# Fewer first-pass chunks for the first two token blocks, later key copies for a new batch, and 1 + exp(-|h|) on ScalarE

## The chip, the cores and the metric

The kernel runs on one core of one Trainium2 chip. A core has TensorE (PE in the profile, its weight loads PEld), VectorE (DVE), ScalarE (ACT), GpSimd (POOL) and SyncE (SP), and 16 DMA engines. Each engine takes its instructions from a queue of its own, in order, and waits on semaphores for what other engines and transfers make. The metric is the device time of one execution in microseconds (us), the median over the runs of a kernel.

## The reference, cut to what matters

Block-sparse attention (4 batches, 8 heads, 768 tokens of 64 elements) feeds a layer with a softplus. A block has 32 rows. A block of queries sees its neighbours, the first and the last block of keys, and three sampled ones; the first and the last block of queries see all keys.

```python
mask = np.abs(blk_i - blk_j) <= 1
mask |= (blk_i == 0) | (blk_j == 0) | (blk_i == n_blocks - 1) | (blk_j == n_blocks - 1)
# and mask[qb, kb] for the three sampled kb of each qb
attn = softmax(where(mask, q @ k.T / 8, -1e9))
x = (attn @ v)                       # 3072 tokens x 512
h = x @ w_in                         # 512 -> 2048
g = maximum(h, 0) + log1p(exp(-abs(h)))
out = g @ w_out                      # 2048 -> 512
```

All of it is in float32. The two weight matrices come as 8-byte numbers, which the kernel turns into float32 itself.

## The kernel before, in words

**Attention.** The tokens of a batch are six groups of 128 queries (three groups make a token block of 384, `GROUPS`, eight token blocks in all, `NTB`). Each group is a set; the queries that see all keys make one more set per batch, ahead of the batch's last group. A set has two units, so there are 28 sets and 56 units, 14 units a batch. A unit goes through scores (PE line 597, or 621 where all keys are seen), a masked minimum on VectorE (603 or 628), the exponents on ScalarE (653), transposes (666), copies of these out of PSUM (671 on VectorE, 673 on ScalarE), and values (696 or 710). In program order this is cut into three pieces a unit (`pieces`): score piece, value piece, transpose piece. `attend()` issues one piece and then calls `gather()` and `convert()`.

**Keys of a group.** The keys of a batch lie in `kT`, one buffer, so a batch's keys can be loaded only after the last scores of the batch before that read them. The score piece of the last all-keys unit issues the four loads of the next batch's keys (`load_kT`, line 427) and then `load_keys()`, which puts four entries (`of_block`) into `key_work`; each later `gather()` takes one of them. `of_block(0)` holds VectorE's copy of the neighbouring keys into the group's own buffer `kg` (line 493) and, for the first two groups of a batch, ScalarE's two copies of the first and the last key block (`end_keys`, line 476); each `of_block` also holds GpSimd's copies of the sampled blocks (507).

**The layer.** It runs in chunks: a chunk is one token block of 384 and one slice `f` of 128 of the 2048 hidden elements (`NF` is 16). Chunk n has 12 matmuls for h (lines 237 to 239), then |h| and exp(-|h|) on ScalarE (241, 242), `rounding` on VectorE (248: u = e + 1; 250 and 251 make max(h, 0) less what the sum lost), the logarithm on ScalarE (256), VectorE's sum (261), ScalarE's high part (265), VectorE's low part (271), and nine matmuls of `project` (293 to 295), `LEAD` = 3 chunks after h. There are 128 chunks in two passes. In the first pass (`phase` 0) every token block takes slices 0 to 5 (`EARLY`), among the pieces of the attention; the second pass takes all the other slices after it. `due` paces the pieces against the chunks: block t's chunks may begin when the attention of its three groups is issued, so the number of chunks of block 0 sets how many chunks stand between the attention of block 0 and that of block 1.

**Weights.** Each of the 32 halves (a slice of `w_in` or of `w_out`) is converted in steps spread over ticks, four ticks a half: ScalarE lines 155 and 159, VectorE 165, 172 and 178, GpSimd 182; the halves of slices 0 to 5 are also split into a high part (ScalarE 189) and a low part (VectorE 196) and stay in SBUF, the others are parked in memory. `convert()` adds to `owed` and does a tick whenever it reaches 1: one tick a call until the twelve early halves are through, half a tick a call from then on.

**What sets the order.** SyncE's queue follows the program text. For the other engines a scheduler orders the instructions by priority and by its own estimate of when each can start, except where `keep_in_program_order` pins one; so a change in the program text moves instructions on all of them.

## Time and profile before

| what | value |
|---|---|
| device time, median of 3 runs | 806.91 us (806.14 to 807.39) |
| device time of the profiled execution | 808.32 us |
| its span, first to last instruction | 806.6 us |
| TensorE busy | 777.5 us, 96% of the span |
| VectorE busy | 579.5 us, 72% |
| ScalarE busy | 490.0 us, 61% |
| GpSimd busy | 223.6 us, 28% |
| mean granted TensorE clock | 0.994 |

The profiled execution took 1.7 us more than its span and 1.4 us more than the median of the runs. A row of the view of groups gives an engine, a line of the kernel, the operation, out<-in by tile names, the count, then busy time and the mean of one in ns, and behind the bar the engine's idle time before these instructions and what ended it. A row of the view of windows gives a stretch from:to in us after the first instruction, its length, busy time and instructions (x) of PE, PEld, DVE, ACT and POOL, the granted clock, the DMA engines' busy share and GB/s. A row of the timeline gives start, length, engine, line, operation, and in brackets the idle time before it and what released it. The busy time of TensorE is modelled at its ends: a matmul that waits inside a run of others is counted as busy.

### The profile page before, as it was taken

What the parts mean: (1) busy time and instruction counts of PE and PEld (TensorE: products, weight loads), DVE (VectorE), ACT (ScalarE), POOL (GpSimd) and SP (SyncE); (2) the same over time, 40 slices, a digit from 0 to 9 for tenths busy, and PEclk for the clock granted to TensorE, in tenths of its full rate; (3) what the DMA queues carried; (4) which work ended last, traced back from release to release, by engine and by line L of the source; (5) the groups of instructions that cost most, each with busy time, mean ns of one, the idle gap of its engine ahead of it and who ended that gap; (6) DMA issues with size and microseconds to landing.
All of it is one profiled execution on the core that took longest, in us unless ns stands there. A gap on an engine that the chain in (4) does not pass through costs nothing.

```text
span 806.6 us, 21414 instructions
## 1 busy us (share of the span) xinstructions
PE 777.5 (96%) x8108; PEld 645.0 (80%) x8108; DVE 579.5 (72%) x1474; ACT 490.0 (61%) x1182; POOL 223.6 (28%) x389
## 2 busy tenths in 40 slices
PE   8788898998999999999999999999999999999997
PEld 7555666776777867778778999989999899988996
DVE  5689899887887888886756975656565656566564
ACT  4887886766877767767565764444444444444442
POOL 6874886625464436663000000000000000000000
PEclk9999999999999999999999999999999999999999
DMA  8999887886697786956415831203040313121021
GB/s 247 265 251 311 217 218 241 246 293 209 190 307 212 257 277 165 283 157 203 154 46 183 298 133 62 96 25 133 1 157 1 119 39 119 39 96 62 0 79 40
DMA packets 48407, 129.65 MB, mean 161 GB/s; under 512 B 5488, under 2 KB 5616, under 8 KB 46256
## 3 DMA queue, kind: packets, MB, share of 16 engines
q1 hardware_dynamic: 42304, 109.79, 42.7%
q0 software_dynamic: 5712, 17.57, 7.7%
q8 instruction: 64, 1.05, 0.5%
q10 hardware_dynamic: 288, 0.93, 0.3%
q14 instruction: 39, 0.32, 0.1%
HBM read 97.85 MB, written 30.41 MB: 159 GB/s over the span
## 4 chain that ended last, share of the span: by engine, by line
PE 72%; DVE 12%; ACT 9%; DMA 3%; issue 2%; SPq 1%; ACTq 0%; DVEq 0%
PE o L293 10%; PE h L237 10%; PE h L238 10%; PE o L294 10%; PE o L295 10%; PE h L239 10%; ACT pr L653 4%; PE t L666 4%; PE s L597 3%; PE x L696 3%; DMA kT<-in_k_dram 2%; DMA vg<-in_v_dram 2%; DVE e L250 2%; DVE pr L603 2%; DVE wt L178 1%
## 5 line engine op out<-in xcount | busy, mean ns | idle before, releaser
L237 PE MATMUL h<-x,w 128*128 128x384 f32 x512 | 176.5, 345 | 1.4 <-ACT pt L673 0.3
L238 PE MATMUL h<-x,w 128*128 128x384 f32 x512 | 172.5, 337 | 0.0
L239 PE MATMUL h<-x,w 128*128 128x384 f32 x512 | 172.4, 337 | 0.0
L293 PE MATMUL o<-w,gh 128*128 128x512 f32 x384 | 155.7, 405 | 0.0
L248 DVE TENSOR_SCALAR u<-e 128x384 f32<-128x384 f32 x128 | 49.6, 387 | 143.7 <-ACT e L242 143.4
L295 PE MATMUL o<-w,gl 128*128 128x512 f32 x384 | 152.4, 397 | 0.0
L294 PE MATMUL o<-w,gh 128*128 128x512 f32 x384 | 152.0, 396 | 0.0
L241 ACT ACTIVATE e<-h 128x384 f32<-128x384 f32 x128 | 62.5, 489 | 128.2 <-PE h L239 127.9
L653 ACT ACTIVATE pr<-pr,nmax 128x256 f32<-128x256 f32 (+2 forms) x208 | 110.3, 532 | 37.5 <-DVE nmax L603 24.3
L563 POOL DMA_INDIRECT vg<-in_v_dram,ix x88 | 90.1, 1023 | 69.2 <-PE x L696 38.0
L265 ACT CAST gh<-u 128x384 fp32r<-128x384 f32 x128 | 65.4, 511 | 69.9 <-PE o L294 69.2
L237 PEld LDWEIGHTS h<-x,w 128*128 128x128 f32 x512 | 96.1, 188 | 11.2 <-DVE nmax L628 2.2
L507 POOL COPY kg<-kT 128x128 f32 x252 | 88.4, 397 | 41.1 <-PE s L597 36.1
L238 PEld LDWEIGHTS h<-x,w 128*128 128x128 f32 x512 | 96.3, 188 | 3.7
L239 PEld LDWEIGHTS h<-x,w 128*128 128x128 f32 x512 | 96.1, 188 | 0.0
L256 ACT ACTIVATE u<-u 128x384 f32<-128x384 f32 x128 | 66.9, 523 | 42.8 <-DVE e L250 42.7
L293 PEld LDWEIGHTS o<-w,gh 128*128 128x128 f32 x384 | 72.1, 188 | 20.7 <-issue 8.6
L295 PEld LDWEIGHTS o<-w,gl 128*128 128x128 f32 x384 | 72.3, 188 | 17.3
L294 PEld LDWEIGHTS o<-w,gh 128*128 128x128 f32 x384 | 72.3, 188 | 13.5 <-issue 1.2
L250 DVE SCALAR_TENSOR_TENSOR e<-u,e 128x384 f32<-128x384 f32 x128 | 77.0, 602 | 3.6
L271 DVE TENSOR_TENSOR gl<-u,gh 128x384 fp32r<-128x384 f32 x128 | 73.2, 572 | 4.5 <-ACT gh L265 4.5
L261 DVE TENSOR_TENSOR u<-u,e 128x384 f32<-128x384 f32 x128 | 72.8, 569 | 3.4 <-ACT u L256 1.7
(81 smaller groups left out, 1082.4 us busy)
## 6 DMA issues: line engine op xcount, KB each, us to landing
vg<-in_v_dram SPq DMA_DIRECT2D x19, 768.0 KB, 6.4
xD<-x SPq DMA_DIRECT2D x8, 1536.0 KB, 7.1
x<-xD SPq DMA_DIRECT2D x8, 1536.0 KB, 6.3
raw<-in_w_in_dram SPq DMA_DIRECT2D x16, 512.0 KB, 9.9
raw<-in_w_out_dram SPq DMA_DIRECT2D x16, 512.0 KB, 8.5
qc<-in_q_dram SPq DMA_DIRECT2D x24, 256.0 KB, 7.1
vg<-in_v_dram SPq DMA_DIRECT2D x12, 512.0 KB, 5.9
yD<-os SPq DMA_DIRECT2D x24, 256.0 KB, 3.5
```

Source lines behind the costliest of these rows:

```text
L237: nc.tensor.matmul(ph, wh[:, cols], hi[:, c], start=(c == 0), stop=False)
L238: nc.tensor.matmul(ph, wh[:, cols], lo[:, c], start=False, stop=False)
L239: nc.tensor.matmul(ph, wl[:, cols], hi[:, c], start=False, stop=(c == NC - 1))
L250: nc.vector.scalar_tensor_tensor(out=e, in0=u, scalar=-1.0, in1=e, op0=ALU.add, op1=ALU.subtract)
L261: nc.vector.tensor_tensor(out=l, in0=l, in1=e, op=ALU.add)
L271: nc.vector.tensor_tensor(out=gl, in0=l, in1=G[n].bitcast(F32), op=ALU.subtract)
L293: nc.tensor.matmul(po[m], gh[:, cols], wh, start=first, stop=False)
L294: nc.tensor.matmul(po[m], gh[:, cols], wl, start=False, stop=False)
L295: nc.tensor.matmul(po[m], gl[:, cols], wh, start=False, stop=last)
L507: copy(out=kd[:, i, 1 + NR + s, :], in_=kT[b][:, bass.ds(x, 1), :].rearrange("p n f -> p (n f)"))
L563: nc.gpsimd.indirect_dma_start(out=vd[0 : 3 * BLOCK, 1, i, :], out_offset=None, in_=v, in_offset=bass.IndirectOffsetOnAxis(ap=ix[:, b, 4 * ...
L653: nc.scalar.activation(x, x, AF.Exp, bias=nmax[rows, r, j : j + 1], scale=-1.0, accum_out=rs[rows, h : h + 1])
```

## The change

Three edits and what they pull along. The first pass gives token block 0 four chunks (`EARLIEST`), block 1 five, and the other six blocks six each, 45 chunks in all where 48 stood; the second pass takes what is left, 83 chunks where 80 stood. The early weight halves are sorted by when this order wants them, and the early rate of conversion is 0.8 ticks a call, until 8 halves are through where 12 were. At a new batch three empty entries stand in `key_work` ahead of the first group's four, and the copies of the first and last key block go with the second entry instead of the first, pinned in program order. In `rounding`, u = 1 + e is made by an activation on ScalarE instead of VectorE's `tensor_scalar_add`.

```diff
+EARLIEST = 4
+ARRIVAL = 3
-EARLY_TICKS = 1.0
+EARLY_TICKS = 0.8
...
-    seq = [(0, t, f) for t in range(NTB) for f in range(EARLY)]
-    seq += [(1, t, f) for t in range(NTB) for f in range(EARLY, NF)]
+    early_of = [min(EARLY, EARLIEST + t) for t in range(NTB)]
+    steps = [sum(early_of[:t]) for t in range(NTB + 1)]
+    seq = [(0, t, f) for t in range(NTB) for f in range(early_of[t])]
+    seq += [(1, t, f) for t in range(NTB) for f in range(early_of[t], NF)]
...
-        nc.vector.tensor_scalar_add(out=u, in0=e, scalar1=1.0)
+        nc.scalar.activation(u, e, AF.Copy, bias=1.0)
...
-        first, last = (f == (0, EARLY)[phase]), (f == (EARLY, NF)[phase] - 1)
+        first, last = (f == (0, early_of[t])[phase]), (f == (early_of[t], NF)[phase] - 1)
...
-            copy(
+            ins = copy(
...
+            if m >= NG:
+                tc.keep_in_program_order(ins)
...
-                if m % NG < 2:
-                    first = nc.vector.tensor_copy if m == 0 else nc.scalar.copy
-                    end_keys(m, (first, nc.scalar.copy))
+            if m % NG < 2 and i == (m >= NG):
+                first = nc.vector.tensor_copy if m == 0 else nc.scalar.copy
+                end_keys(m, (first, nc.scalar.copy))
...
+        if g == 0 and b > 0:
+            key_work.extend((m, lambda: None) for _ in range(ARRIVAL))
...
-    early = sorted(((f, which) for f in range(EARLY) for which in range(2)), key=lambda x: (x[0] + LEAD * x[1], x[1]))
+    def wanted_at(f):
+        t = max(0, f + 1 - EARLIEST)
+        return steps[t] + f
+
+    early = sorted(
+        ((f, which) for f in range(EARLY) for which in range(2)), key=lambda x: (wanted_at(x[0]) + LEAD * x[1], x[1])
+    )
...
-    SECOND = NTB * EARLY
+    SECOND = steps[NTB]
...
-        owed += EARLY_TICKS if weights.at < 4 * len(early) + 9 else LATE_TICKS
+        owed += EARLY_TICKS if weights.at < 8 * EARLIEST + 9 else LATE_TICKS
...
-            end = t * EARLY - AHEAD
+            end = steps[t] - AHEAD
```

The change shifts the line numbers: lines 241, 242, 248, 250, 251, 256 of before are 248, 249, 255, 257, 258, 263 of after; 476 is 483, 493 is 502, 603 is 614, 653 is 664, 673 is 684; the weights' 155, 159, 165, 172, 178, 189, 196 are 159, 163, 169, 176, 182, 193, 200.

Three places show what the scheduler makes of it. First VectorE between the minimum of unit 14 (`nmax14`) and that of unit 15, in batch 1's first group, before. `wt` and `w1` tiles are weights, e3, u3 and h3 belong to chunk 3:

```order
L603 ISA nmax14_1797 128x1
L248 TENSOR_SCALAR u3_1862<-e3_1794 128x384
L759 TENSOR_TENSOR x0_1_1350<-y5_1833,x0_1_1350 128x4x64
L250 SCALAR_TENSOR_TENSOR e3_1794<-u3_1862,e3_1794 128x384
L251 SCALAR_TENSOR_TENSOR e3_1794<-h3_1781,e3_1794 128x384
L165 TENSOR_SCALAR wt14_1855<-wt14_1855 128x512
L172 TENSOR_SCALAR wt14_1855<-wt14_1855 128x512
L178 SCALAR_TENSOR_TENSOR wt14_1855<-raw14_1580,wt14_1855 128x512
L196 TENSOR_TENSOR w112_1896<-wt12_1643,w012_1895 128x512
L603 ISA pr15_0_1901,nmax15_1900<-s15_0_1903,mask_156 128x256
```

The same stretch of VectorE's queue after:

```order
L614 ISA nmax14_1734 128x1
L770 TENSOR_TENSOR x0_1_1325<-y5_1770,x0_1_1325 128x4x64
L257 SCALAR_TENSOR_TENSOR e2_1731<-u2_1853,e2_1731 128x384
L258 SCALAR_TENSOR_TENSOR e2_1731<-h2_1718,e2_1731 128x384
L200 TENSOR_TENSOR w111_1797<-wt11_1452,w011_1796 128x512
L614 ISA pr15_0_1819,nmax15_1818<-s15_0_1821,mask_156 128x256
```

Between the two units one whole half's conversion and the addition of 1 are gone from VectorE, and the chunk that stands there is chunk 2 instead of chunk 3.

Second ScalarE at the arrival of batch 1's keys (`kT1`), before, from the exponents of unit 11 (`pr11`) to those of unit 12:

```order
L653 ACTIVATE pr11_1_1426,sums10_1342<-pr11_1_1426,nmax11_1424 128x768
L155 ACTIVATE wt05_1513<-raw05_1223 128x512
L476 COPY kg0_178<-kT1_1445 128x4x128
L673 COPY pt10_0_1525<-t10_0_1524 128x512
L673 COPY pt10_8_1539<-t10_8_1538 128x512
L159 ACTIVATE raw05_1223<-raw05_1223 128x512
L189 CAST w004_1582<-wt04_1307 128x512
L256 ACTIVATE u1_1516<-u1_1516 128x384
L653 ACTIVATE pr12_0_1561,sums12_1607<-pr12_0_1561,nmax12_1560 64x256
L476 COPY kg0_178<-kT1_1445 128x4x128
L189 CAST w010_1467<-wt10_1177 128x512
L241 ACTIVATE e2_1604<-h2_1591 128x384
```

The same of after, from chunk 1's 1 + e (line 255, the new instruction) on:

```order
L255 ACTIVATE u1_1617<-e1_1470 128x384
L193 CAST w010_1644<-wt10_1315 128x512
L766 CAST x0_1_1325<-y4_1542 128x4x128
L664 ACTIVATE pr12_0_1506,sums12_1537<-pr12_0_1506,nmax12_1505 64x256 x2
L664 ACTIVATE pr12_1_1507,sums12_1537<-pr12_1_1507,nmax12_1505 64x256 x2
L483 COPY kg0_178<-kT1_1410 128x4x128 x2
L684 COPY pt11_0_1579<-t11_0_1578 128x512
```

Both copies of the end keys now stand behind all four exponents of unit 12; the first of them stood one unit earlier and the second among those exponents.

Third VectorE's copy of the neighbouring keys, before: it stands ahead of the minimum of unit 12.

```order
L725 RECIPROCAL sums10_1342<-sums10_1342 128x4
L493 COPY kg0_178<-kT1_1445 128x4x384
L671 COPY pt10_4_1532<-t10_4_1531 128x512
L165 TENSOR_SCALAR wt05_1513<-wt05_1513 128x512
L603 ISA pr12_0_1561,nmax12_1560<-s12_0_1563,mask_156 64x256
```

After, it stands behind it:

```order
L614 ISA pr12_1_1507,nmax12_1505<-s12_1_1509,mask_156 64x256
L614 ISA nmax12_1505 64x1
L502 COPY kg0_178<-kT1_1410 128x4x384
L257 SCALAR_TENSOR_TENSOR e1_1470<-u1_1617,e1_1470 128x384
L770 TENSOR_TENSOR x0_1_1325<-y4_1542,x0_1_1325 128x4x128
```

The copy moved from ahead of one unit's minimum to behind it, about one unit later.

## The prediction

> **What bounds the kernel now.** I read the page's busy times first, then the windows, then the chain inside two of them. The page:
>
> ```profile
> span 806.6 us, 21414 instructions
> PE 777.5 (96%) x8108; PEld 645.0 (80%) x8108; DVE 579.5 (72%) x1474; ACT 490.0 (61%) x1182; POOL 223.6 (28%) x389
> ```
>
> TensorE is the limit on average, but the average hides the stages. I cut the span where VectorE's minimum of units 8, 11, 18, 24, 28, 38, 42 and 55 ended (lines 603, 628), so that the same attention work can be found in both programs. The windows (busy PE, PEld, DVE, ACT, POOL); the first begins at unit 0's minimum:
>
> ```profile
> 17.70:55.70 38.00, 30.33 (x748) 19.99 (x748) 29.14 (x101) 32.16 (x93) 31.72 (x60) 0.96 0.91 251
> 55.70:75.20 19.50, 17.49 (x295) 11.21 (x297) 17.54 (x51) 15.00 (x38) 7.38 (x7) 1.00 0.94 316
> 75.20:133.00 57.80, 50.55 (x744) 37.52 (x732) 55.06 (x143) 45.04 (x118) 45.86 (x68) 0.97 0.88 247
> 133.00:179.10 46.10, 45.22 (x680) 34.68 (x683) 37.86 (x106) 32.42 (x90) 20.56 (x31) 1.00 0.76 238
> 179.10:213.80 34.70, 31.76 (x450) 24.51 (x448) 27.67 (x77) 25.37 (x62) 15.62 (x32) 1.00 0.65 201
> 213.80:286.70 72.90, 72.38 (x1138) 56.18 (x1140) 59.80 (x174) 52.77 (x146) 38.25 (x64) 1.00 0.85 259
> 286.70:319.40 32.70, 32.54 (x461) 25.57 (x460) 26.62 (x76) 25.04 (x62) 17.51 (x33) 1.00 0.68 210
> 319.40:415.70 96.30, 94.95 (x1477) 73.85 (x1476) 70.95 (x211) 64.02 (x176) 35.34 (x61) 1.00 0.58 175
> ```
>
> From 75 to 133 us VectorE is busy 55.06 of 57.80 us (95%); later TensorE is, 98 or 99% in most rows. The chain of waits agrees: the first row is of 84 to 134 us, the second of 200 to 260 us.
>
> ```profile
> by line: DVE pr L603 13.7%; DVE w L196 9.4%; DVE wt L178 9.2%; DVE e L250 7.2%; DVE sums L724 6.4%; DVE kg L493 5.7%; issue 5.7%; DVE wt L165 5.3%; DVE wt L172 4.8%; DVE u L248 4.5%; DVE e L251 4.3%; DVE u L261 3.9%; DVE pt L671 3.3%; DVE g
> by line: PE t L666 12.1%; PE s L597 12.0%; PE x L696 10.3%; PE h L237 9.3%; PE o L293 8.3%; PE h L239 8.2%; PE h L238 8.1%; PE o L294 7.3%; PE o L295 7.0%; ACT pr L653 3.5%; PE x L710 2.6%; PE y L741 2.1%; ACT raw L159 2.0%; DVE x L759 1.2%
> ```
>
> So an operation off VectorE pays between 75 and 133 us; later it pays little. The number of chunks comes from the count of line 237 (four a chunk), and the price of a chunk from a stretch that holds nothing else:
>
> ```profile
> 55.70:75.20 19.50, 2.88 (x8) 1.50 (x8) 1.00 0.94 316
> 75.20:133.00 57.80, 7.20 (x20) 3.75 (x20) 0.97 0.88 247
> 133.00:179.10 46.10, 8.58 (x24) 4.51 (x24) 1.00 0.76 238
> 480.00:780.00 300.00, 96.56 (x286) 53.72 (x287) 1.00 0.20 69
> ```
>
> In the last row 286 are 71.5 chunks in 300 us: 4.20 us a chunk.
>
> **The change part by part.** The durations, of VectorE's lines that the change thins out and of ScalarE's:
>
> ```profile
> L165 DVE TENSOR_SCALAR wt<-wt 128x512 f32<-128x512 f32 x32 | 14.3, 447 | 8.5 <-ACT wt L155 8.4
> L172 DVE TENSOR_SCALAR wt<-wt 128x512 int32<-128x512 int32 x32 | 13.8, 431 | 0.3
> L178 DVE SCALAR_TENSOR_TENSOR wt<-raw,wt 128x512 int32<-128x512 int32 x32 | 23.1, 721 | 0.4
> L196 DVE TENSOR_TENSOR w<-wt,w 128x512 fp32r<-128x512 f32 x12 | 9.3, 778 | 2.8 <-ACT w L189 2.8
> L248 DVE TENSOR_SCALAR u<-e 128x384 f32<-128x384 f32 x128 | 49.6, 387 | 143.7 <-ACT e L242 143.4
> L250 DVE SCALAR_TENSOR_TENSOR e<-u,e 128x384 f32<-128x384 f32 x128 | 77.0, 602 | 3.6
> L251 DVE SCALAR_TENSOR_TENSOR e<-h,e 128x384 f32<-128x384 f32 x128 | 71.0, 555 | 3.5
> L261 DVE TENSOR_TENSOR u<-u,e 128x384 f32<-128x384 f32 x128 | 72.8, 569 | 3.4 <-ACT u L256 1.7 <-DVE e L251 0.9
> L271 DVE TENSOR_TENSOR gl<-u,gh 128x384 fp32r<-128x384 f32 x128 | 73.2, 572 | 4.5 <-ACT gh L265 4.5
> L155 ACT ACTIVATE wt<-raw 128x512 f32<-128x512 f32 x32 | 21.6, 674 | 0.0
> L159 ACT ACTIVATE raw<-raw 128x512 int32<-128x512 uint32 x32 | 21.8, 682 | 0.0
> L189 ACT CAST w<-wt 128x512 fp32r<-128x512 f32 x12 | 7.4, 615 | 0.0
> L241 ACT ACTIVATE e<-h 128x384 f32<-128x384 f32 x128 | 62.5, 489 | 128.2 <-PE h L239 127.9
> L242 ACT ACTIVATE e<-e 128x384 f32<-128x384 f32 x128 | 67.2, 525 | 3.6
> ```
>
> *Up to 55.7 us.* In the order VectorE loses one each of 165, 172 and 196, 1.66 us, of a stretch that it fills to 77%. Between 0 and -1.7 us; I take -0.5, since the stretch is one of waiting in turn rather than of a full engine.
>
> *55.7 to 75.2 us.* One 165, one 172, two 178 and one 248 go: 2.7 us of VectorE's 17.54, which fill 90% of the stretch. 14.8 at 90% is 16.5, or -3.0. I take -2.5; TensorE loses one of the two chunks and is no bar.
>
> *75.2 to 133 us.* By the order VectorE loses two each of 165, 172 and 178 (3.2), three of 196 (2.3), six of 248 (2.3) and two each of 250, 251, 261 and 271 (4.6): 12.5 us. Left are 42.6, at the same 95% 44.7 us: -13.1. ScalarE loses two each of 155 and 159 and three of 189 (4.6) and of the chunks' operations one each of 241 and 242 and two each of 256 and 265 (3.1, the last two at 525), and gains four additions: no row shows an addition there, so it lies between 489 (241) and 525 ns (242), and I take 525, since 242 too reads SBUF: 2.1 us. Its 45.0 become 39.4, no bar. TensorE's 50.55 lose one chunk of the five: 46.3, which would be a bar if its modelled busy time is all work. I take -11, 46.8 us. Within this stretch the copy's wait for the new keys goes too; these rows of the timeline show what it costs now, from the issue of the loads on SyncE:
>
> ```profile
> 74.64 1.76 SPq L427 DMA_DIRECT2D kT<-in_k_dram  x4
> 83.83 0.62 ACT L476 COPY kg<-kT 128x512 f32<-128x512 f32 x1 [2.44 <-DMA kT<-in_k_dram]
> 84.02 5.45 POOL L507 COPY kg<-kT 128x128 f32 x15 [3.10 <-DMA kT<-in_k_dram]
> 85.00 0.69 DVE L196 TENSOR_TENSOR w<-wt,w 128x512 fp32r<-128x512 f32 x1 [2.17 <-ACT w L189]
> 87.89 1.12 PE L666 MATMUL t<-ident,pr 128*128 128x128 f32 x4 [2.34 <-DVE e L251]
> 188.26 0.96 DVE L493 COPY kg<-kT 128x1536 f32<-128x1536 f32 x1 [1.67 <-DMA kT<-in_k_dram]
> 192.83 0.62 ACT L476 COPY kg<-kT 128x512 f32<-128x512 f32 x1 [0.93 <-DMA kT<-in_k_dram]
> ```
>
> ScalarE stands for the keys, a weight's high part and chunk 2's |h| stand behind it, VectorE waits 2.17 us for the one, and TensorE stands 2.34 us. With the copies behind unit 12's exponents the keys have landed. What is late next would be GpSimd: its sampled copies are needed three units after the loads, about 20 us at 46.8 us for seven units. They begin when the keys land, 84.0 - 74.6 = 9.4 us after the issue, and take 5.5: some 5 us to spare. If that cover went, TensorE would wait for GpSimd.
>
> The halves that wait move on SyncE's queue (their loads and parking) and on GpSimd's (line 182) by the same ticks; I cost that at nothing, since in the order slice 4 is split four chunks before block 1 asks for it. If that lead were gone, TensorE would wait for the weights at chunk 8.
>
> *133 to 179.1 us.* Full on TensorE; one of six chunks leaves. -4.2 at most; four 196 and 189 are added here, so -3.5.
>
> *179.1 to 213.8 us.* The second arrival: VectorE waits 1.67 and ScalarE 0.93 us, TensorE is not busy for 2.9. Between 0 and -2.9; -2. *286.7 to 319.4 us*, the third: TensorE shows next to no idle time there. Between 0 and the second's 1.7; -1, since that busy time is modelled.
>
> *213.8 to 286.7 and 319.4 to 415.7 us.* Full on TensorE, same chunks. Four weight halves come late, into the second: 4 x (674 + 682) ns of ScalarE and 11 additions, 11.2 us on 64.02, 78% of the stretch; VectorE gains 6.4 and loses 4.3. In the first ScalarE gains nine additions, 4.7 us. TensorE's work hides all of this while neither engine holds an exponent or a copy back. I take +1.5, between -1 and +5.
>
> *After the attention.* Three chunks more stand alone, 3 x 4.20: +12.6. Here ScalarE's extra 0.525 us a chunk is covered by the 4.2 of TensorE, and VectorE's loss gains nothing.
>
> Sum: -0.5 - 2.5 - 11 - 3.5 - 2 - 1 + 1.5 + 12.6 = -6.4 us. The profiled span of 806.6 becomes 800.2; the median of the runs, 806.91, becomes 800.5. A measurement of this kernel can tell about 0.2% (1.6 us) from no change.
>
> Here a rule speaks against the change. The Trainium skill (ScalarE: Activation LUTs, Rules for kernel authors) says to put additions on VectorE, not on ScalarE. The rows agree on the price of one, 387 against 489 to 525 ns. By that rule 128 x 138 ns, 17.7 us of engine time, would be lost; the windows decide otherwise where VectorE is the full engine, and it becomes the second rival below where it is not.
>
> **The rivals.** *Nothing net (806.5).* The three chunks are 12.6 us of TensorE's work taken out of the attention; they pay only if the attention shortens by more. If units 11 to 18 are next held by the turns between ScalarE and VectorE, and shorten by 5 instead of 11, the sum is -0.4. For: in the first row of the windows a unit takes 4.75 us (38 us for eight) with no engine over 85% busy, so waiting in turn has its own price. Against: the chain from 84 to 134 us is VectorE almost alone. That the scheduler undoes the edits is ruled out by the order.
>
> *ScalarE becomes late (811.7, slower).* From 179 to 416 us ScalarE gets 26 additions by the order, 13.7 us, and the late halves' 5.4: 19.1 on 167.2 busy, in order ahead of the exponents for which TensorE's transposes wait. If two thirds reach TensorE, 12.7 us instead of the 1.5 that I count, the sum is +4.8. It decides from the point where 41% reach it, 7.9 us. For: exponents are 3.5% of the chain even where TensorE is full. Against: ScalarE would still be at 79%.
>
> *More (793.4).* The stretches shrink to VectorE's bound and the waits go whole: -1.7 - 2.5 - 13.1 - 4.2 - 2.9 - 1.7 + 0 + 12.6 = -13.5. Against: it needs TensorE's busy time in the early units to be part waiting.
>
> *The clock drops (803.9).* Behind the gap of 2.34 us the granted clock falls, for 85 to 90 and 90 to 95 us:
>
> ```profile
> 85.00:90.00 5.00, 2.66 (x14) 1.69 (x16) 4.89 (x10) 4.71 (x13) 5.00 (x13) 0.76 0.76 194
> 90.00:95.00 5.00, 5.00 (x80) 3.91 (x73) 5.00 (x13) 5.00 (x15) 5.00 (x8) 0.90 0.56 179
> ```
>
> That is 5 x 0.24 + 5 x 0.10 = 1.7 us of clock lost. With fewer chunks to fill them, gaps between unit 8 and 24 may grow; two such drops more cost 3.4 us, and the sum is -3.0. The Trainium skill (TensorE: Matmul & The Clock Gate, Why this matters for your kernels) warns of gaps of over about 3 us between bursts; by that rule the trace's 2.34 us is near the edge.
>
> **How the numbers follow.** The forecast has 0.45, more 0.17, the clock 0.08, nothing net 0.13, ScalarE late 0.17. Faster: 0.45 + 0.17 + 0.08 = 0.70; within 0.2%: 0.13; slower: 0.17. The range of 794 to 807.5 leaves out half of "more" and about two thirds of "late", some 0.2, and takes in nothing net and the bounds of the forecast's own terms.
>
> **What would show it.** In the profile after, the chunks after the attention should still take 4.20 us each and begin some 19 us earlier. Units 11 to 18 should take 45 to 48 us with VectorE near 90%; no wait of ScalarE's or VectorE's for kT should be left at the three arrivals, and none of TensorE's for GpSimd's copies. The addition should show 489 to 525 ns. I am wrong if those units take over 52 us, or if the stretches from 179 to 416 us grow by over 8 us, with exponents in the chain.

## The result, and the profile after

The change makes the kernel slower: 813.18 us (median of 8 runs, 810.61 to 817.07) beside 807.15 us for the kernel before (8 runs, 805.40 to 811.48), a ratio of 1.0064 [1.0035, 1.0092]. The forecast was 800.5 us; the range reached to 807.5. A few executions of these kernels ran in a slower state of the chip and are left out of every ratio; the profiled one of the run "chunks only" below was among them, so its stretches are not given. The profiled execution has a span of 813.5 us where 806.6 stood. Its page:

```profile
span 813.5 us, 21427 instructions
PE 780.7 (96%) x8108; PEld 648.2 (80%) x8108; DVE 540.9 (66%) x1346; ACT 552.6 (68%) x1310; POOL 217.3 (27%) x389
```

VectorE has lost 38.6 us of work and ScalarE gained 62.6; the 128 additions now on it are 67.2 us. TensorE still shows 96%. The windows of after, cut at the same minima as those of before (units 0, 8, 11, 18, 24, 28, 38, 42 and 55):

```profile
18.00:55.60 37.60, 31.22 (x747) 20.56 (x748) 27.32 (x97) 30.36 (x90) 28.83 (x58) 0.91 0.87 233
55.60:73.60 18.00, 15.37 (x295) 9.64 (x294) 15.81 (x49) 13.50 (x35) 6.94 (x8) 1.00 1.03 353
73.60:125.40 51.80, 42.87 (x691) 32.28 (x689) 44.82 (x117) 40.43 (x108) 38.37 (x66) 0.97 0.93 246
125.40:170.80 45.40, 43.23 (x660) 32.62 (x662) 36.73 (x103) 34.60 (x95) 20.70 (x31) 0.96 0.70 208
170.80:202.80 32.00, 30.98 (x448) 24.19 (x446) 26.85 (x73) 26.47 (x63) 15.69 (x32) 1.00 0.73 229
202.80:277.60 74.80, 73.71 (x1143) 56.63 (x1145) 58.29 (x167) 56.88 (x157) 38.08 (x64) 1.00 0.83 251
277.60:310.90 33.30, 32.43 (x456) 25.19 (x455) 24.98 (x70) 26.14 (x64) 17.87 (x33) 1.00 0.73 218
310.90:410.10 99.20, 95.85 (x1481) 74.03 (x1480) 74.95 (x211) 72.99 (x197) 39.28 (x65) 1.00 0.65 198
410.10:813.50 403.40, 399.10 (x2051) 358.07 (x2049) 221.57 (x426) 243.54 (x499) 0.00 (x0) 1.00 0.24 87
```

Set beside the rows of before, length by length:

| stretch | before | after | difference | forecast |
|---|---|---|---|---|
| to unit 8 | 55.7 | 55.6 | -0.1 | -0.5 |
| units 8 to 11 | 19.5 | 18.0 | -1.5 | -2.5 |
| units 11 to 18 | 57.8 | 51.8 | -6.0 | -11 |
| units 18 to 24 | 46.1 | 45.4 | -0.7 | -3.5 |
| units 24 to 28 | 34.7 | 32.0 | -2.7 | -2 |
| units 28 to 55 | 201.9 | 207.3 | +5.4 | +0.5 |
| behind unit 55 | 390.9 | 403.4 | +12.5 | +12.6 |

The attention ends 5.6 us earlier instead of 19, and the three chunks behind it cost what was said. Part of what happened to the other 13 us shows where the second batch's keys arrive. The timeline of after, SyncE's loads and the copies that wait for them:

```profile
72.14 2.00 SPq L434 DMA_DIRECT2D kT<-in_k_dram  x4
84.07 0.62 ACT L483 COPY kg<-kT 128x512 f32<-128x512 f32 x1 [0.70 <-DMA kT<-in_k_dram]
84.16 10.54 POOL L516 COPY kg<-kT 128x128 f32 x24 [4.31 <-DMA kT<-in_k_dram]
```

The loads are issued 2.5 us earlier than before (72.14 against 74.64), and GpSimd's copies begin at 84.16, where they began at 84.02. From the issue to these copies it is 12.0 us where it was 9.4, while the DMA engines are full in units 8 to 11 (share 1.03, 353 GB/s; before 0.94, 316). By this reading, what the lighter units gain is lost to a stream of transfers that comes no sooner. ScalarE's wait shrank from 2.44 to 0.70 us, as the later copies meant, but GpSimd's grew from 3.10 to 4.31. The chain of waits, first of after's 73.6 to 125.4 us, then of 125.4 to 170.8 us:

```profile
by line: DMA kT<-in_k_dram 19.9%; ACT pr L664 13.2%; DVE w L200 7.7%; issue 7.6%; DVE pr L614 4.7%; DVE e L257 3.8%; ACT wt L159 3.6%; DVE wt L169 3.5%; ACT kg L483 3.2%; PE t L677 2.9%; PE s L608 2.7%; DVE wt L182 2.5%; PE x L707 2.4%; ACT
by line: ACT pr L664 12.4%; PE s L608 9.5%; PE x L707 7.3%; PE t L677 6.8%; PE h L244 6.1%; PE h L245 5.9%; PE h L246 5.8%; PE o L300 5.5%; PE s L632 5.3%; PE o L302 4.7%; PE o L301 4.6%; ACT pt L684 3.2%; ACT x L766 2.3%; PE y L752 2.3%; A
```

The same two stretches of before, 75.2 to 133.0 and 133.0 to 179.1 us:

```profile
by line: DMA kT<-in_k_dram 13.6%; DVE pr L603 11.9%; DVE w L196 8.1%; DVE wt L178 7.9%; DVE e L250 6.2%; DVE sums L724 5.6%; issue 5.0%; DVE kg L493 4.9%; DVE wt L165 4.6%; DVE wt L172 4.1%; DVE u L248 3.9%; DVE e L251 3.7%; DVE u L261 3.4%
by line: ACT pr L653 9.0%; PE t L666 8.3%; PE x L696 7.6%; PE s L597 6.7%; PE h L237 6.1%; PE h L239 6.1%; PE h L238 6.0%; PE o L293 5.9%; DVE e L250 4.8%; PE o L295 4.6%; DVE u L248 4.6%; PE o L294 4.5%; PE s L621 3.6%; issue 2.7%; DVE e L
```

The prediction's chain of 84 to 134 us began when the keys were there and so left their transfer out. Cut like that of after, the chain of before has it in front as well, 13.6% of 57.8 us; in after it is 19.9% of 51.8 us, behind it stand the exponents (13.2%) and no longer VectorE's minimum. In units 18 to 24 the exponents are the largest single line in both kernels, 9.0% and 12.4%, and TensorE's lines together are some 60% in both: that stretch was not TensorE's alone before the change either. That the engines wait for each other in turns there is read from these rows; no run isolates it. The groups of the addition and of the line behind it:

```profile
L257 DVE SCALAR_TENSOR_TENSOR e<-u,e 128x384 f32<-128x384 f32 x128 | 81.1, 634 | 181.5 <-ACT u L255 181.1
L255 ACT ACTIVATE u<-e 128x384 f32<-128x384 f32 x128 | 67.2, 525 | 4.1 <-DVE gl L278 0.7 <-DVE sums L735 0.2
```

An addition on ScalarE takes 525 ns, the value taken.

### The profile page after: what moved, and what is told of

It is laid out like the page before. It is cut to its first block, busy times and chain, and to the rows that moved or that the text cites. A ratio compares the mean times of both kernels' runs of the same rounds, so it can differ in the third digit from the quotient of the medians.

```text
span 813.5 us, 21427 instructions
## 1 busy us (share of the span) xinstructions
PE 780.7 (96%) x8108; PEld 648.2 (80%) x8108; DVE 540.9 (66%) x1346; ACT 552.6 (68%) x1310; POOL 217.3 (27%) x389
## 4 chain that ended last, share of the span: by engine, by line
PE 71%; ACT 13%; DVE 9%; DMA 3%; issue 3%; SPq 0%; POOL 0%; POOLq 0%; ACTq 0%; DVEq 0%
PE h L244 10%; PE o L300 10%; PE h L245 10%; PE h L246 10%; PE o L302 10%; PE o L301 10%; ACT pr L664 6%; PE s L608 4%; PE t L677 3%; PE x L707 3%; DMA vg<-in_v_dram 2%; DVE e L257 1%; ACT pt L684 1%; DVE pr L614 1%; DMA kT<-in_k_dram 1%
## 5 line engine op out<-in xcount | busy, mean ns | idle before, releaser
L257 DVE SCALAR_TENSOR_TENSOR e<-u,e 128x384 f32<-128x384 f32 x128 | 81.1, 634 | 181.5 <-ACT u L255 181.1
L244 PEld LDWEIGHTS h<-x,w 128*128 128x128 f32 x512 | 97.1, 190 | 12.9 <-DVE nmax L639 2.9
L574 POOL DMA_INDIRECT vg<-in_v_dram,ix x88 | 87.8, 998 | 57.5 <-PE x L707 28.7
L245 PEld LDWEIGHTS h<-x,w 128*128 128x128 f32 x512 | 97.2, 190 | 3.8
L246 PEld LDWEIGHTS h<-x,w 128*128 128x128 f32 x512 | 97.2, 190 | 0.0
L516 POOL COPY kg<-kT 128x128 f32 x252 | 85.0, 383 | 42.0 <-PE s L608 35.6
L301 PEld LDWEIGHTS o<-w,gh 128*128 128x128 f32 x384 | 72.2, 188 | 13.2 <-issue 0.8
L608 PE MATMUL s<-kg,qc 64*32 64x256 f32 x1408 | 64.1, 388 | 11.2 <-DVE x L770 4.9
```

Of the source, the lines that this page charges most:

```text
L244: nc.tensor.matmul(ph, wh[:, cols], hi[:, c], start=(c == 0), stop=False)
L245: nc.tensor.matmul(ph, wh[:, cols], lo[:, c], start=False, stop=False)
L246: nc.tensor.matmul(ph, wl[:, cols], hi[:, c], start=False, stop=(c == NC - 1))
L257: nc.vector.scalar_tensor_tensor(out=e, in0=u, scalar=-1.0, in1=e, op0=ALU.add, op1=ALU.subtract)
L301: nc.tensor.matmul(po[m], gh[:, cols], wl, start=False, stop=False)
L516: copy(out=kd[:, i, 1 + NR + s, :], in_=kT[b][:, bass.ds(x, 1), :].rearrange("p n f -> p (n f)"))
```

## The experiments

Four theories are told apart. The trade: a chunk costs 4.20 us behind the attention and earns less inside, so moving three out is the loss. ScalarE late: the additions hold exponents back. The clock: fewer chunks leave gaps, and TensorE is throttled behind them. The weights: the slower rate of conversion brings halves late. In the recorded expectations the first is F (filler), the second S, the third C; I says that the edits interact, and T (turns) says why a chunk would earn little inside: a unit's own way through the engines sets its pace. Chips differ: before takes 807 us in the first runs and 808 on one chip later, 820 to 823 on three others, where units 0 to 8 take 46 us instead of 38 in before again. So a ratio is to runs of before on the same chip, and stretches are compared within a chip or between chips of one kind. All stretches of this table are cut from one trace of each run at the same minima, in us; where a kernel was profiled twice on chips of one kind, they differ by up to 1.8 us:

| run | median | ratio to before | 8-11 | 11-18 | 18-24 | 24-28 | 28-55 | behind |
|---|---|---|---|---|---|---|---|---|
| before again | 821.21 | 0.9988 [0.9964, 1.0012] | 21.5 | 58.7 | 46.8 | 32.6 | 205.0 | 390.8 |
| addition only | 820.08 | 0.9979 [0.9949, 1.0008] | 21.4 | 57.6 | 46.0 | 32.2 | 205.1 | 390.9 |
| keys only | 825.16 | 1.0034 [1.0009, 1.0058] | 22.6 | 54.8 | 47.3 | 32.8 | 207.0 | 390.8 |
| keys, addition | 817.53 | 0.9936 [0.9909, 0.9963] | 20.5 | 54.1 | 45.2 | 32.5 | 208.1 | 390.8 |
| the same again | 816.67 | 0.9958 [0.9929, 0.9988] | 21.1 | 54.5 | 45.2 | 32.6 | 207.2 | 390.8 |
| chunks only | 833.48 | 1.0104 [1.0056, 1.0153] | | | | | | |
| chunks, keys | 832.11 | 1.0109 [1.0071, 1.0147] | 21.9 | 48.6 | 48.9 | 32.8 | 210.3 | 403.7 |
| chunks, addition | 831.81 | 1.0131 [1.0089, 1.0174] | 20.2 | 52.6 | 51.6 | 31.9 | 207.7 | 403.5 |
| chunks only, old rate | 827.70 | 1.0070 [1.0045, 1.0096] | 21.1 | 53.0 | 48.2 | 32.7 | 206.8 | 404.8 |
| after, old rate | 829.96 | 1.0099 [1.0066, 1.0133] | 18.9 | 51.8 | 48.4 | 34.3 | 208.9 | 404.0 |
| after again | 831.59 | 1.0140 [1.0096, 1.0183] | 19.3 | 49.8 | 51.3 | 32.6 | 210.1 | 403.4 |
| after, third time | 831.53 | 1.0110 [1.0072, 1.0149] | 18.9 | 49.2 | 53.1 | 32.6 | 209.7 | 404.1 |

**The parts apart.** The addition alone is one line:

```diff
-        nc.vector.tensor_scalar_add(out=u, in0=e, scalar1=1.0)
+        nc.scalar.activation(u, e, AF.Copy, bias=1.0)
```

> Kernel before with 1 + exp(-|h|) on ScalarE and nothing else. Theory S (ScalarE late: the addition stands in order ahead of exponents and copies, and the stretch from unit 28 to 55 grows by some 5 us): 810 to 814 us against 807 of before, that stretch longer by 4 us or more. Theory F (filler: the three chunks taken out of the attention cost more than the attention shortens, the addition is harmless): 804 to 807 us, units 11 to 18 shorter by 1 to 2 us, units 28 to 55 within 1.5 us of before.

0.9979, and units 28 to 55 take 205.1 us as in before again (205.0). ScalarE's 128 additions cost nothing there: its lateness falls as a theory. Moving them also gains little, 1.1 us in units 11 to 18.

The chunks alone: `EARLIEST`, `EARLY_TICKS`, `steps`, `early_of` and `wanted_at` of the change, without its other two edits.

> Kernel before with four, five, then six chunks in the first pass and the 0.8 rate of weight conversion, and nothing else. Theory S: 801 to 805 us: units 8 to 24 shorter by 15 us or more, 12.6 us given back at the end. Theory F: 810 to 814 us: units 8 to 24 shorter by 7 to 10 us only, 12.6 us given back at the end, and the granted clock drops as often as in the kernel after (four times ahead of the end, twice before).

1.0104: this edit carries the loss. Theory F's times are 0.4 to 0.9% over the 807 us of before, so it is F's side, and a little more.

The copies of a new batch's keys alone:

```diff
+            if m % NG < 2 and i == (m >= NG):
+                first = nc.vector.tensor_copy if m == 0 else nc.scalar.copy
+                end_keys(m, (first, nc.scalar.copy))
...
+        if g == 0 and b > 0:
+            key_work.extend((m, lambda: None) for _ in range(ARRIVAL))
```

> Kernel before with the later copies of a new batch's keys and nothing else. Both theories: 804 to 807 us; no wait of VectorE's neighbour copy for the new keys is left, and units 24 to 28 are 1 to 3 us shorter.

1.0034, where no loss was expected. Against before again units 11 to 18 are 3.9 us shorter, units 28 to 55 2.0 longer and 8 to 11 1.1 longer; units 24 to 28, expected 1 to 3 us shorter, take the same (32.8 against 32.6). The moved copies pay at the first arrival, not at the second, and these units later take longer.

Two edits at a time: the change with the addition back on VectorE,

```diff
-        nc.scalar.activation(u, e, AF.Copy, bias=1.0)
+        nc.vector.tensor_scalar_add(out=u, in0=e, scalar1=1.0)
```

> Kernel after with the addition back on VectorE. Theory S: 799 to 804 us, 10 us under the kernel after, units 28 to 55 as in before. Theory F: 808 to 813 us, within 3 us of the kernel after, with the chunks' 12.6 us at the end not earned by units 0 to 24.

with the key copies back in their place,

```diff
...
-        if g == 0 and b > 0:
-            key_work.extend((m, lambda: None) for _ in range(ARRIVAL))
```

> Kernel after with the key copies back where they stood. Theory F (the chunks cost some 8 us, the addition gains 1 to 2, the keys cost 1 to 3): 0.5 to 0.9% over before. Theory S is down after the first runs; a third, I (the edits interact, no single one carries the loss), would put it at before or under.

and with six chunks a block, the old order of the weights and the old rate back:

```diff
-    seq = [(0, t, f) for t in range(NTB) for f in range(early_of[t])]
+    seq = [(0, t, f) for t in range(NTB) for f in range(EARLY)]
...
```

> Kernel after with six chunks for every block and the old conversion, so the addition and the keys alone. Theory F: within 0.3% of before, 5 us or more under the kernel after. Theory I: 0.5% or more over before.

Both pairs with the chunks are slower by over 1%, the second by more than F gave; the pair without them has the lowest ratio of the study, 0.9936. It gains more than F gave too: alone the two edits have 0.9979 and 1.0034, so together they gain what neither gains alone, and why is open. To know how much a ratio may wander, before itself:

> The kernel before once more, for its profile beside the others of this call on the same chip. Both theories: the time of before within 0.3%; it gives the length of units 8 to 24 and 28 to 55 with which the others are compared.

0.9988, within the interval of no change.

**The rate.** The chunks alone, converted as before:

```diff
-EARLY_TICKS = 0.8
+EARLY_TICKS = 1.0
...
-        owed += EARLY_TICKS if weights.at < 8 * EARLIEST + 9 else LATE_TICKS
+        owed += EARLY_TICKS if weights.at < 4 * len(early) + 9 else LATE_TICKS
```

> Four, five, then six chunks, but the weights converted at the old rate (1 tick a call until twelve halves are through); keys and addition as in before. It tells the moved chunks from the deferred weights. If the loss of the chunks edit is the filler (12.6 us at the end, not earned by units 8 to 24, which stay bound by VectorE): 0.8 to 1.4% over before. If it is the late weight halves in units 46 to 55 (some 3 us) and those units' turns: 0.4% or less over before, units 46 to 55 as in before.

1.0070: still slower, between what the two theories gave. Against before again on the same chip, units 8 to 24 are 4.7 us shorter without the three chunks and units 28 to 55 1.8 longer.

**The clock.** The change with two matmuls of the identity, into scratch that the transposes overwrite, ahead of each group of four transposes in units 8 to 23, to fill gaps:

```diff
+            for i in range(2 if 8 <= n < 24 else 0):
+                nc.tensor.matmul(ps[:, i], ident, ident, start=True, stop=True)
```

> Kernel after with two extra matmuls of the identity ahead of each group of four transposes in units 8 to 23 (some 70 of 0.22 us, 15 us of TensorE in all; they write where the transposes write next, so nothing is left of them). Theory C (the clock: the removed chunks leave gaps in which TensorE's clock is halved, and that is what lengthens units 8 to 24): none or one halved stretch of the clock between unit 8 and 24, those units 3 us or more shorter than in the kernel after, and 0.4% or more under it. Theory T (turns: a unit's own chain through VectorE, ScalarE, TensorE and GpSimd sets its pace, the clock is a symptom): the clock stays up, but units 8 to 24 are no shorter, and the time is that of the kernel after or up to 1% over it.

1.0253. The windows of its units 11 to 18 and 18 to 24:

```profile
86.20:138.60 52.40, 46.87 (x744) 37.18 (x743) 41.41 (x120) 41.12 (x109) 38.00 (x66) 0.99 0.89 247
138.60:189.70 51.10, 49.25 (x715) 39.23 (x717) 35.47 (x101) 35.07 (x94) 20.40 (x31) 0.97 0.60 185
```

The granted clock is nearly whole, but the stretches are no shorter than in the same kernel without the fillers on that chip (49.8 and 51.3). The clock alone did not hold them. The 136 fillers add 22.1 us to TensorE's busy time, so a smaller share of the clock isn't excluded.

**More chunks out.** The chunks alone at the old rate again, with

```diff
-EARLIEST = 4
+EARLIEST = 2
```

so blocks take two, three, four, five, then six chunks: ten move.

> As the kernel with chunks alone at the old rate of conversion, but two, three, four, five, then six chunks in the first pass: 10 chunks moved to the end instead of 3, 42 us added there. Theory T: a moved chunk earns some 1.5 us in the attention, as measured with three: 3% to 3.6% over before. If VectorE's load sets the pace (2.7 us of it a chunk): 1.5% to 2.2% over before. If TensorE's load does (4.2 us a chunk): within 0.5%.

1.0345 [1.0302, 1.0388] for 847.69 us. Units 8 to 24 take 108.5 us instead of before again's 127.0 (-18.5 for seven chunks fewer), units 28 to 55 208.5 instead of 205.0 with two fewer; behind, 433.1 instead of 390.8. Ten chunks cost 42.3 us outside and earned 16.1 inside, 1.6 each, as theory T had it.

**The addition only early.** Keys and addition, the latter on ScalarE for the first 24 chunks alone:

```diff
+        if n < 24:
+            nc.scalar.activation(u, e, AF.Copy, bias=1.0)
+        else:
+            nc.vector.tensor_scalar_add(out=u, in0=e, scalar1=1.0)
```

> The keys and the addition alone, with the addition on ScalarE for the first 24 chunks (VectorE's full stretch) and on VectorE from there on. If the addition on ScalarE costs in the later units: 0.2% or more under the keys and the addition for all chunks, so 0.9% or more under before. If it is harmless there: within 0.3% of it, 0.3% to 0.9% under before.

0.9960 [0.9934, 0.9985] with units 28 to 55 at 208.5: the additions there are not what lengthened them, and nothing is gained by sparing them. Beside it ran the change:

> The kernel after once more, for its profile and ratio beside the others of this call on the same chip. All theories: 0.3% to 1.2% over before.

1.0140.

**No chunk inside.** All 128 chunks are put behind the attention, in one pass; the stored partial sums fall away, and the weights are all converted before the first chunk:

```diff
-    seq = [(0, t, f) for t in range(NTB) for f in range(EARLY)]
-    seq += [(1, t, f) for t in range(NTB) for f in range(EARLY, NF)]
+    seq = [(1, t, f) for t in range(NTB) for f in range(NF)]
...
```

> Kernel before with all of the attention ahead of all 128 chunks (one pass of 16 chunks a block; the partial sums are not parked in memory). Its units show the attention's own pace, with the weights' conversion and no chunk. If a chunk among the attention is charged what it takes from TensorE (4.2 us), units 28 to 55 take some 108 us, where 205 stand with 23 chunks; if VectorE's share is charged (2.7 us), some 143 us; if the units' own turns set the pace and the chunks ride along, 180 us or more. For units 8 to 24, 127 us with 13 chunks: 72, 92 or 115 us and more.

The whole takes 907.67 us, 1.1216 [1.1146, 1.1285] beside 807.72, but what counts is the attention without chunks. Its windows, of units 8 to 11, 11 to 18, 18 to 24 and 28 to 55, and behind them the chain of units 8 to 24:

```profile
56.50:73.30 16.80, 13.29 (x279) 8.04 (x279) 13.57 (x44) 11.53 (x30) 5.73 (x6) 0.90 1.03 341
73.30:121.10 47.80, 33.31 (x628) 22.85 (x628) 35.39 (x105) 32.52 (x91) 36.20 (x64) 0.86 0.85 239
121.10:153.80 32.70, 25.31 (x566) 15.82 (x564) 24.53 (x78) 22.57 (x68) 23.73 (x34) 0.95 1.04 275
182.30:337.00 154.70, 123.97 (x2584) 83.39 (x2582) 97.81 (x334) 94.99 (x281) 86.51 (x159) 0.89 0.91 264
```

```profile
by line: DMA vg<-in_v_dram,ix 16.8%; DMA vg<-in_v_dram 14.0%; DMA kT<-in_k_dram 9.2%; issue 8.7%; PE s L596 5.3%; PE x L695 4.9%; POOL kg L506 4.6%; PE t L665 4.2%; POOL wt L182 4.0%; DVE pr L602 3.8%; PE s L620 3.7%; POOLq L506 2.6%; DVE w
```

No engine is over 81% busy, yet units 8 to 18 take 64.6 us; the transfers of keys and values are 40% of the chain (16.8 + 14.0 + 9.2) and the DMA engines are 85 to 104% busy. Units 28 to 55 take 154.7 us and units 8 to 24 97.3: in both, of the three values expected, the one by VectorE's share (143 and 92) is nearest, and the turns of theory T (180 and 115) are too long. Against before on a chip of the same kind the attention ends 78.7 us earlier (337.0 against 415.7) for 39 chunks: 2.0 us a chunk. That is what a chunk earns inside on the average, against 4.20 outside.

**Chunks in, instead of out.** Seven a block, with keys and addition. To make room for two more halves, the raw weights get two buffers instead of four, so six with two buffers stands beside it:

```diff
-EARLY = 6
+EARLY = 7
...
-    weights = Weights(early + later, 3, 4)
+    weights = Weights(early + later, 3, 2)
```

> The keys and the addition alone, with seven chunks a block in the first pass instead of six: eight more chunks lie among the attention or right behind it, seven of them among it. The memory for the two more weight halves comes from two of the four raw weight buffers. Theory T turned round: a chunk among the attention costs some 2.7 us there and saves 4.2 at the end, so 7 x 1.5, some 10 us or 1.2%, under the same kernel with six chunks and two raw buffers, if the weights still come in time. If the attention is already full on TensorE: within 0.3% of it.

> The keys and the addition alone with two raw weight buffers instead of four, six chunks a block: what the next kernel is compared with. If the shorter lead of the weights' loads costs nothing: 0.4% to 0.9% under before, as with four. If it costs: up to 1% over before.

825.45 and 818.81 us, ratios 1.0206 [1.0164, 1.0248] and 1.0125 [1.0089, 1.0161]. Six chunks more inside save 25.2 us behind (365.6 against 390.8) and lengthen units 8 to 55 by 30.9 (401.2 against 370.3): 5.2 us each. So seven is not 1.2% under six, as theory T had it, but 0.8% over it (825.45 against 818.81 us). Moving the other way doesn't pay either; how much of the 5.2 is late weights is open, since ScalarE waits for raw halves in both.

**Rate or chunks, on one chip.** The last three share a chip and their runs of before.

> The kernel before with the later key copies and the addition on ScalarE, run a second time, beside the next two on one chip. If the gain of the first time (0.9936) is the edits' own: 0.992 to 0.996, attention about 4 to 6 us shorter, 390.8 us behind it. If it belonged to that chip, whose units before 8 took 8 us longer: 0.998 to 1.002.

> The change as it is, beside the other two. 1.004 to 1.016 by the two times before. Against the run of keys and addition on the same chip the chunks' edit with its slower conversion should cost 1.0 to 2.0% if the edits' prices add; under 0.6% if they do not.

> The change with the old rate of conversion, 1.0 ticks a call until 12 halves are through. If the slower rate is what spoils the last units (late halves in units 46 to 55) and the prices add (0.9936 x 1.007): 0.998 to 1.003, units 28 to 55 some 3 us shorter than in the change. If the rate is innocent and the moved chunks do all: the change's own ratio within 0.3%, units 28 to 55 the same.

816.67, 831.53 and 829.96 us. The old rate changes the change by 0.2%, inside the intervals, and units 28 to 55 by 0.8 us: the theory of the weights falls as the cause of the loss. What is left between keys and addition and the change, 13 to 15 us, goes with the moved chunks and the order of the weight halves that comes with them. The windows of keys and addition, units 8 to 11, 11 to 18, 18 to 24, 24 to 28 and 28 to 55:

```profile
63.90:85.00 21.10, 19.87 (x343) 13.71 (x342) 17.65 (x51) 17.84 (x44) 7.19 (x6) 0.92 0.86 279
85.00:139.50 54.50, 50.57 (x734) 37.77 (x724) 50.91 (x133) 46.09 (x122) 46.24 (x68) 0.97 0.91 265
139.50:184.70 45.20, 44.62 (x679) 34.27 (x682) 36.42 (x102) 35.55 (x95) 20.07 (x32) 1.00 0.72 227
184.70:217.20 32.50, 31.40 (x449) 24.43 (x450) 26.29 (x74) 26.19 (x63) 16.25 (x32) 1.00 0.75 231
217.20:424.40 207.20, 202.07 (x3070) 156.40 (x3069) 150.75 (x433) 152.74 (x406) 89.08 (x158) 1.00 0.69 206
```

The same five of the change, beside it on that chip:

```profile
64.50:83.40 18.90, 17.28 (x329) 11.77 (x330) 15.89 (x47) 14.43 (x37) 6.08 (x6) 0.91 0.96 312
83.40:132.60 49.20, 42.26 (x660) 31.06 (x659) 42.41 (x117) 40.35 (x109) 36.40 (x64) 0.90 0.88 243
132.60:185.70 53.10, 48.10 (x688) 35.74 (x690) 36.36 (x102) 34.86 (x94) 23.28 (x34) 0.94 0.66 189
185.70:218.20 32.50, 31.37 (x449) 24.44 (x450) 26.28 (x74) 26.18 (x63) 16.23 (x32) 1.00 0.72 227
218.20:428.00 209.80, 203.57 (x3070) 156.58 (x3069) 157.86 (x445) 156.54 (x415) 95.53 (x162) 1.00 0.71 218
```

Units 8 to 18 are 7.5 us shorter with the chunks out, and units 18 to 24 are 7.9 longer, though they are full (44.62 of 45.20 at a clock of 1.00) only where the chunks stay. Unit 24 ends at 184.7 and 185.7 us. Everything that the moved chunks earned is given back in one stretch. At the old rate it is spread: units 8 to 18 take 70.7 us, units 18 to 24 48.4, and units 24 to 55 3.4 us more than with keys and addition. The timelines of both, of the one and then of the other, show at the keys' loads again that the keys come no sooner for being asked for sooner:

```profile
84.41 1.75 SPq L429 DMA_DIRECT2D kT<-in_k_dram  x4
92.28 7.65 POOL L511 COPY kg<-kT 128x128 f32 x18 [0.67 <-DMA kT<-in_k_dram]
```

```profile
81.96 2.63 SPq L434 DMA_DIRECT2D kT<-in_k_dram  x4
92.39 8.10 POOL L516 COPY kg<-kT 128x128 f32 x17 [2.73 <-DMA kT<-in_k_dram]
...
135.31 0.53 PE L707 MATMUL x<-vg,pt 128*32 128x64 f32 x19 [4.17 <-issue]
```

Two of its windows around that last row:

```profile
130.00:135.00 5.00, 1.14 (x48) 0.85 (x47) 4.44 (x16) 4.00 (x12) 4.37 (x4) 1.00 1.06 277
135.00:140.00 5.00, 4.69 (x34) 3.73 (x34) 1.82 (x3) 0.59 (x2) 0.15 (x1) 0.66 0.52 116
```

Issued 2.45 us earlier, the copies begin 0.1 us later. And where the change has come ahead, at 131 us, TensorE stands 4.17 us before a product with the gathered values, with the DMA engines full (share 1.06); behind that gap the granted clock is 0.66 for five microseconds. That it waits there for the gather to land is argued from what the product reads; the profile names no releaser.

## Why the prediction was wrong

*The three chunks behind.* Right: 12.5 us against 12.6.

The span came out 13.3 us over the forecast sum (+6.9 against -6.4): 5.0 of it are units 11 to 18, 4.9 units 28 to 55, 2.8 units 18 to 24, 1.0 units 8 to 11.

*Units 11 to 18, -11.* This step failed: -6.0. It took VectorE's 95% for the only limit and shortened the stretch in proportion. The attention alone, with no chunk, takes 16.8 + 47.8 = 64.6 us for units 8 to 18; the forecast gave 17.0 + 46.8 = 63.8 with only two of their seven chunks gone. VectorE's work did leave, 10.2 us of the 12.5 reckoned (55.06 to 44.82), but four tenths of that time stayed as waiting. A bar stood in the quoted rows, in the column that I didn't use: before, the DMA engines' share of 0.94 and 0.88 is 69 us of transfers in these 77. That the transfers hold the stretch is argued, not shown: no run here takes them out, and in the rows with shares of 0.93 to 1.06 the rate lies anywhere between 246 and 354 GB/s. What I set against "nothing net", that the chain was VectorE almost alone, came from a window that began behind the keys' transfer, and it only told who came last. That rival named these units' outcome, -5 by turns; what it missed is that the other terms fail too.

*Units 18 to 24, -3.5.* Failed: -0.7, and on the other kind of chip 4.5 and 6.3 us longer than before again (51.3 and 53.1 against 46.8). "Full on TensorE" was a busy time modelled at 98%, while the chain of these units had the exponents in front already. A chunk out left TensorE 43.23 of 45.40 us (95%): by this reading the chunk had worked in what would else be waits. The Trainium skill (Perfetto Trace Analysis, Identifying the Most-Contended Engine) warns that the matmul busy share is not a good measure of how close TensorE is to its limit, and points to the share of weight loads. The rows agree, though their matmuls are not of the same shapes: behind the attention of after PEld fills 358.07 of 403.4 us (89%), in units 18 to 24 of before 34.68 of 46.10 (75%).

*Units 24 to 28, -2, and the first arrival.* Right in the number, -2.7, but that the later copies earned it is not shown. In before again VectorE waits 1.83 us for these keys:

```profile
200.64 0.96 DVE L493 COPY kg<-kT 128x1536 f32<-128x1536 f32 x1 [1.83 <-DMA kT<-in_k_dram]
```

Yet the stretch is 32.6 us there, and 32.5 to 32.8 us in the three runs that move the copies without the chunks; only the first profile of before has the 34.7 us that the change is measured from. At the first arrival ScalarE's wait did go from 2.44 to 0.70 us. GpSimd's cover did not hold as I reckoned it: its copies begin when the keys land, 12.0 us after the issue and not 9.4.

*Units 28 to 55, +0.5.* Failed: +5.4. The parts: later key copies +2.0 (keys only), the addition +0.1, both +2.2 and +3.1; the moved chunks 2.6 more on the chip of the last three (209.8 against 207.2), of which 0.8 go at the old rate, no more than the two traces of keys and addition differ (208.1 and 207.2). Why later copies lengthen these units wasn't tried.

*ScalarE late, 0.17 of the chances.* Its total (811.7) came near the result by luck: the addition alone lengthens nothing there. The prediction's own two signs of being wrong did not show either: units 11 to 18 took 51.8 us, not over 52, and the stretches from 179 to 416 us grew by 2.7, not by over 8. They looked for one stretch that fails, and four fell short by a little.

*The clock.* The clock lost is about that rival's 3.4 us, though its total (803.9) was far off: the span's mean is 0.991 where before had 0.994, some 3.5 us more of TensorE's time up to unit 24 by the windows' clock (37.6 x 0.09 + 51.8 x 0.03 + 45.4 x 0.04 = 6.8, against 3.3 before). It accompanies the gaps; filling them, on the other kind of chip, gained nothing.

The root is one price. The forecast let three chunks' moved work earn as if the stretches were each set by one full engine. Measured, a chunk earns 2.0 us when all 39 leave, 1.6 when ten do, 0.9 for these three at the old rate (361.9 against 364.5 us for units 8 to 55), and nothing beside keys and addition (362.3 against 360.6). It costs 4.20 behind. How far the transfers, the turns and the clock share in this is open.

## What to carry to other kernels

Work that fills the waits of another stage gives back less than its own length when it is taken out: here 2.0 us a chunk or less, against 4.20 alone. That doesn't make room for more of it, since six more cost 5.2 us each, late weights included. Price it by a run of that stage without any filling, before counting on a busy engine's share. Cut both programs at the same marks and see whether a gain in one stretch is given back in the next. Read the DMA column beside the engines' before calling an engine the limit: here a transfer issued 2.5 us earlier landed at the same time.

## What the runs showed of the hardware

A stand of TensorE of under 3 us can be followed by a lower clock. The first of these windows of after holds one of 2.63 us, the second what was granted behind it:

```profile
110.00:115.00 5.00, 2.09 (x72) 1.28 (x72) 4.71 (x13) 4.03 (x11) 3.15 (x8) 1.00 1.06 354
115.00:120.00 5.00, 4.83 (x43) 4.74 (x44) 4.44 (x10) 2.90 (x9) 4.38 (x9) 0.66 0.91 286
```

The timeline at that place:

```profile
115.17 0.54 PE L707 MATMUL x<-vg,pt 128*32 128x64 f32 x24 [2.63 <-issue]
```

PE is busy for 2.09 of 5 us in the first, and the clock is 0.66 in the second. The Trainium skill (TensorE: Matmul & The Clock Gate, Why this matters for your kernels) sets the mark at about 3 us; here 2.63 sufficed, in a stretch that was more than half idle. The length of the stand doesn't decide by itself. In before one of 2.20 us had no drop behind it:

```profile
132.42 1.31 PE L666 MATMUL t<-ident,pr 128*128 128x128 f32 x8 [2.20 <-DVE nmax L603]
130.00:135.00 5.00, 2.74 (x33) 2.40 (x22) 4.38 (x13) 3.38 (x12) 1.17 (x1) 1.00 1.04 295
135.00:140.00 5.00, 5.00 (x110) 3.52 (x108) 3.75 (x14) 3.54 (x10) 3.03 (x11) 1.00 0.25 73
```

In after one of 1.72 us had, although TensorE was busier around it:

```profile
128.46 1.09 PE L608 MATMUL s<-kg,qc 64*32 64x256 f32 x30 [1.72 <-DVE x L770]
125.00:130.00 5.00, 3.28 (x43) 1.89 (x42) 3.74 (x11) 4.52 (x14) 0.35 (x1) 0.98 0.57 148
130.00:135.00 5.00, 5.00 (x81) 4.53 (x81) 4.07 (x13) 3.12 (x11) 4.48 (x13) 0.68 0.02 5
```

An addition of VectorE took four times its usual length beside additions of GpSimd. The timeline of after:

```profile
96.84 3.33 DVE L200 TENSOR_TENSOR w<-wt,w 128x512 fp32r<-128x512 f32 x1 [0.23 <-ACT w L193]
97.05 2.56 POOL L186 TENSOR_TENSOR wt<-wt,raw 128x512 int32<-128x512 int32 x2
```

It takes 778 ns on the mean (line 196 of before), here 3.33 us, across two additions of GpSimd of 1.3 us. Of its twelve executions in after the five that took 1.2 us or more all overlap such an addition; the other seven took 0.67 to 0.69 us. The Trainium skill (SBUF — State Buffer, Who interferes with whom) says that the two engines share a pair of ports and that an instruction of VectorE with two inputs in SBUF contends with one of GpSimd that reads SBUF; the trace agrees. This instruction began 0.21 us ahead of GpSimd's first addition and still ended last; an indirect DMA instruction of GpSimd was running until 97.03 us, so the trace doesn't tell which of the two engines came first.
